# The last 64 positions of the first batch's values, loaded first as 512-byte runs on 16 partitions and summed in one block on TensorE

## Chip, cores and metric

The kernel runs on one core of one Trainium2 chip. The metric is the time of one execution on the device in microseconds (us). Nearly all executions of one kernel lie within 2 us of each other; a few are 7 to 16 us longer at a lower granted TensorE clock (0.98 or 0.99 in the mean). Those are called slow here, and only undisturbed executions are compared.

## The reference

```python
def _attn_ref(q, k, v):                    # each (8, 8, 576, 64) float32: batch, head, position, dim
    pool, scale = 8, 1.0 / np.sqrt(64)
    k_p = k.reshape(B, H, S // 8, 8, D).mean(axis=3)      # 72 pooled keys per head
    v_p = v.reshape(B, H, S // 8, 8, D).mean(axis=3)      # 72 pooled values per head
    scores = scale * np.matmul(q, k_p.transpose(0, 1, 3, 2))
    scores = scores - np.max(scores, axis=-1, keepdims=True)
    attn = np.exp(scores)
    attn = attn / (np.sum(attn, axis=-1, keepdims=True) + 1e-09)
    return np.matmul(attn, v_p)

def _moe_ref(x, w_gate, w_val, w_out):     # x (4608, 512), d_ff 1536
    return (np.maximum(x @ w_gate, 0.0) * (x @ w_val) @ w_out)

# x = the attention's output, (batch, position) as rows and (head, dim) as columns
```

The kernel casts to 16-bit floats on the way in, pools keys and values, and keeps TensorE on the feed-forward part as early and as long as it can.

## The kernel before

Two ways of pooling values are in it. For batches 2 and up, GpSimd sums eight positions with trees of adds. For the first two batches it is done on TensorE: the values lie with positions on the partitions, and a 0/1 matrix (`sel_main`, `sel_rest`) sums eight of them per output row. 576 positions are 144 runs of KG = 4 positions. 128 of these runs (512 positions) fill 128 partitions, the "main" values. The last 64 positions, the "rest", were loaded one position to a partition, on 64 partitions. In the code P = 128, SP = 72 pooled positions, HH = 4 heads (half of them), NKG = 9, and QP = 16.

```python
    def load_v_wide(b):
        tl = vin_pool.tile([P, H, POOL, D], F16, name="v_in")
        main = tl[:, :H // 2].rearrange("p h t d -> p (h t d)").rearrange(
            "p (h t d) -> p h t d", h=H, d=D)
        rest = tl[:P // 2, H // 2:].rearrange("p h t d -> p (h t) d")[:, :H]
        v_tiles[b] = (main, rest)
        nc.gpsimd.dma_start(
            out=main.rearrange("p h t d -> p h (t d)"),
            in_=v[b].rearrange("h (x t) d -> x h (t d)", t=KG)[:P])
        nc.gpsimd.dma_start(
            out=rest, in_=v[b].rearrange("h r d -> r h d")[P * KG:])
    # ... (cut)
    def warm(n):                      # dummy matmuls that keep the array busy
        ps = ps_mm.tile([P, TCH], F32, name="mm_ps", tag="mm_ps")
        for _ in range(n):
            nc.tensor.matmul(out=ps, lhsT=warm_sb[:, :P], rhs=warm_sb, start=True, stop=True)
    # ... (cut)
    def pool_v_array(b, half):
        ps = ps_mm.tile([P, HH, D], F32, name="mm_ps", tag="mm_ps")
        main, rest = v_tiles[b]
        hs = slice(half * HH, (half + 1) * HH)
        for t in range(KG):
            nc.tensor.matmul(
                out=ps[:SP], lhsT=sel_main, rhs=main[:, hs, t, :], start=(t == 0), stop=False)
        nc.tensor.matmul(
            out=ps[:SP], lhsT=sel_rest[:P // 2], rhs=rest[:, hs, :], start=False, stop=True)
        g0 = half * NG // 2
        st = stats[b % 2][:SP, g0:g0 + NG // 2, :]
        st = st.rearrange("p g (x d) -> p g x d", d=D)[:, :, 0::3, :]
        src = ps[:SP].rearrange("p (g x) d -> p g x d", x=2)
        nc.scalar.copy(st, src)       # the "cast": PSUM float32 to SBUF 16 bit
    # ... (cut) the start of the program, in this order:
        load_k_wide(0, 3)
        make_identity(nc, ident16)
        load_q(0, 0, IQ)
        load_v_wide(0)
        load_gv(0)                    # weights of the gate and value products
        load_q(0, IQ, NI - IQ)
        for i in range(1, 4):
            load_gv(i)
    # ... (cut)
        q_transposes(0, 0, nc.scalar)
        k_turn(k_ps, (3, 7, 8, 4))
        k_take(0, k_ps, False)
        k_take(0, k_ps, True)
        warm(2)
        piece_scores(0)               # exp(q k_p) of the first two pieces of 128 queries
        warm(2)
        piece_scores(1)
        warm(4)
        pool_v_array(0, 0)
        pool_v_array(0, 1)
    # ... (cut)
        values(0, 0)                  # products with the pooled values, reciprocal, multiply
        values(0, 1)
        warm(1)
        back(0, 0, nc.scalar)         # transposes into x_T, the feed-forward's input
```

Three parts further on matter for two of the experiments. GpSimd issues all loads of a batch from within its own stream of pooling adds. The third batch's q is transposed by a DMA that SP issues. VectorE forms sums of the output weights:

```python
    def q_dma(b):
        qT_tiles[b] = qT_pool.tile([P, NI, P], F16, name="qT")
        nc.sync.dma_start_transpose(
            out=qT_tiles[b], in_=q16_tiles[b].rearrange("p (i d) -> p i d", d=P))

    def prep_k(b, load_next, behind=None):
        for i in range(KJ // 2):
            run(pool_k(b, i, nc.gpsimd))              # a tree of adds
        if behind is not None:
            nc.gpsimd.tensor_copy(out=gate, in_=behind)
        if load_next:
            load_k(b + 1)
            load_q(b + 1)
            load_v(b + 1)

    def weight_sums():
        e, f = wo_sb[:, :n_hf, :HD], wo_sb[:, :n_hf, HD:]
        g, h = wo_sb[:, n_hf:, :HD], wo_sb[:, n_hf:, HD:]
        t1, t2, t3, t4 = [wo_sums[:, i] for i in range(4)]
        return [lambda o=o, x=x, y=y, i=slice(i, i + 2): nc.vector.tensor_tensor(
                    out=o[:, i], in0=x[:, i], in1=y[:, i], op=ALU.subtract)
                for o, x, y in ((t1, f, e), (t2, h, t1), (t3, h, f), (t4, g, t2))
                for i in range(0, n_hf, 2)]
```

The softmax here doesn't subtract the row's maximum and nothing guards it: scores larger than these inputs give would overflow.

## Time and profile before

| | before |
|---|---|
| time, three runs | 328.61 us median (328.54 to 330.12) |
| span in the profile | 327.4 us |
| TensorE busy | 318.7 us, 97% of the span |
| first load of q landed | 8.88 us |
| main values landed / last 64 positions landed | 12.27 / 12.75 us |
| first value product / VectorE's first reciprocal | 14.45 / 14.79 us |

The page's first part gives each engine's busy time, the chain of waits gives the work that ended last, and the timeline of one engine gives start, duration, engine, line, operation, tiles and count of each group; a bracket at a line's end is idle time just before it and what ended it. The landings come from the trace's records of the DMA engines: a load has landed when the last of its 16 engines has reported. The lines are in the prediction below. The change touches 4 to 17 us, and there TensorE sums values, ScalarE casts the sums, and VectorE takes the value products.

### The profile page before, as it was taken

The page shows a single profiled execution, that of the slowest core. Times are in us where ns is not written, and L with a number is a line of the kernel's source. Part 1 is how long each engine was busy: PE and PEld are TensorE (multiplying, and loading weights), DVE is VectorE, ACT ScalarE, POOL GpSimd, SP SyncE. Part 2 cuts the span into 40 slices and gives each one's busy share as a digit, 9 for nine tenths or more (in the row PEclk, how much of TensorE's full clock was granted, in tenths as well). Part 3 has the DMA queues.
Part 4 walks back from the last instruction along what each step waited for, and adds up shares of the span by engine and source line. Part 5 has one row for each costly group of instructions (what it writes and reads, how often), then busy time and mean ns, then how long its engine had stood idle before and what let it go on. Part 6 is the DMA issues. An engine that isn't in the chain of part 4 may idle for free.

```text
span 327.4 us, 7013 instructions
## 1 busy us (share of the span) xinstructions
PE 318.7 (97%) x2670; PEld 226.9 (69%) x2670; DVE 226.2 (69%) x482; ACT 151.2 (46%) x353; POOL 206.9 (63%) x258
## 2 busy tenths in 40 slices
PE   8899999999999999999999999999999999999995
PEld 3577885455566656665898867655667888888674
DVE  7465737677684864696387745784779989879762
ACT  1454482364466226612672257225825565565330
POOL 8556607999999942965199309999901577667300
PEclk9999999999999999999999999999999999999999
DMA  7999998996958538999794472223012130130035
GB/s 110 186 203 202 200 211 151 200 173 118 187 101 159 100 91 86 78 154 160 159 169 76 87 104 60 33 47 124 3 24 50 34 96 2 22 111 2 10 112 137
DMA packets 51010, 35.46 MB, mean 108 GB/s; under 512 B 30432, under 2 KB 45024, under 8 KB 50976
## 3 DMA queue, kind: packets, MB, share of 16 engines
q0 software_dynamic: 18304, 18.88, 36.5%
q1 hardware_dynamic: 32528, 16.00, 26.2%
q8 instruction: 21, 0.34, 0.4%
q10 hardware_dynamic: 144, 0.13, 0.1%
q14 instruction: 13, 0.11, 0.1%
HBM read 37.75 MB, written 9.44 MB: 144 GB/s over the span
## 4 chain that ended last, share of the span: by engine, by line
PE 89%; DVE 6%; DMA 2%; issue 1%; POOL 1%; ACT 0%; DVEq 0%; POOLq 0%
PE mm_ps L430 42%; PE acc_ps L523 19%; PE mm_ps L742 9%; PE at_ps L311 4%; PE mm_ps L468 3%; PE at_ps L389 3%; PE mm_ps L602 2%; DMA q<-in_q_dram 2%; PE at_ps L742 2%; DVE px L395 1%; DVE sum L514 1%; DVE h L439 1%; PE mm_ps L412 1%; PE mm_ps L366 1%; DVE px L758 1%
## 5 line engine op out<-in xcount | busy, mean ns | idle before, releaser
L439 DVE TENSOR_TENSOR h<-mm_ps,relu 128x512 f16<-128x512 f32 (+1 forms) x96 | 59.8, 624 | 69.5 <-PE mm_ps L430 59.2
L436 ACT ACTIVATE relu<-mm_ps 128x512 f16<-128x512 f32 (+1 forms) x96 | 52.2, 544 | 100.1 <-PE mm_ps L430 94.6
L430 PE MATMUL mm_ps<-x_T,wv_sb 128*128 128x512 f16 (+1 forms) x432 | 88.4, 332 | 0.4 <-DVE kpT0u L264 0.4
L430 PE MATMUL mm_ps<-x_T,wg_sb 128*128 128x512 f16 (+1 forms) x432 | 88.5, 331 | 0.0
L430 PEld LDWEIGHTS <-wv_sb 128*128 128x128 f16 x432 | 42.1, 98 | 31.2 <-DVE kpT0u L264 0.8
L430 PEld LDWEIGHTS <-wg_sb 128*128 128x128 f16 x432 | 38.9, 97 | 19.7 <-issue 0.3
L325 ACT ACTIVATE expT<-at_ps 72x288 f16<-72x288 f32 (+2 forms) x128 | 38.8, 374 | 14.3 <-PE at_ps L311 14.2
L523 PEld LDWEIGHTS <-sum 128*128 128x128 f16 x336 | 32.0, 98 | 6.3 <-DVE sum L514 0.9
L395 DVE TENSOR_TENSOR px<-at_ps,prd 128x256 f16<-128x256 f32 (+1 forms) x80 | 33.8, 423 | 2.7
L181 POOL TENSOR_TENSOR tree_b<-tree_a 72x256 f32<-72x256 f32 (+1 forms) x42 | 33.5, 797 | 3.3
L764 POOL TENSOR_TENSOR h<-px 128x256 f16<-128x256 f16 x36 | 25.4, 718 | 13.8 <-ACT px L761 12.8
L175 POOL TENSOR_TENSOR tree_a<-k_in 96x512 f32<-96x512 f16 x18 | 21.5, 1196 | 15.2 <-DMA k_in<-in_k_dram 15.2
L523 PE MATMUL acc_ps<-wo_sums,sum 128*128 128x256 f16 x252 | 30.9, 272 | 0.0
L175 POOL TENSOR_TENSOR tree_a<-v_in 72x512 f32<-72x512 f16 x24 | 28.7, 1197 | 0.1
L523 PEld LDWEIGHTS <-h 128*128 128x128 f16 x252 | 23.7, 98 | 2.9
L763 POOL TENSOR_SCALAR px<-px 128x256 f16<-128x256 f16 x12 | 13.0, 1080 | 18.1 <-PE mm_ps L742 15.3
L844 POOL COPY gate<-h 128x1 f16<-128x1 f16 x4 | 1.5, 380 | 33.9 <-DVE h L439 33.9
L523 PE MATMUL acc_ps<-wo_sb,h 128*128 128x256 f16 x168 | 20.6, 272 | 0.0
L514 DVE TENSOR_TENSOR sum<-h 128x768 f16<-128x768 f16 x28 | 19.0, 679 | 0.0
L531 DVE TENSOR_TENSOR rows<-acc_ps,mid 128x512 f32<-128x512 f32 x21 | 14.4, 686 | 4.7 <-PE acc_ps L523 4.6
L389 PEld LDWEIGHTS <-expT 72*128 72x128 f16 (+1 forms) x280 | 12.9, 100 | 5.9 <-DVE prd L394 0.8
L394 DVE RECIPROCAL prd<-at_ps 128x4 f32<-128x4 f32 (+1 forms) x80 | 13.7, 171 | 3.7 <-PE at_ps L389 3.6
(144 smaller groups left out, 527.9 us busy)
## 6 DMA issues: line engine op xcount, KB each, us to landing
out_dram<-rows SPq DMA_DIRECT2D x24, 256.0 KB
k_in<-in_k_dram POOLq DMA_DIRECT2D x7, 576.0 KB, 7.0
q<-in_q_dram POOLq DMA_DIRECT2D x7, 576.0 KB, 10.0
v_in<-in_v_dram POOLq DMA_DIRECT2D x6, 576.0 KB, 12.7
wg_sb<-in_moe_w_gate_dram POOLq DMA_DIRECT2D x6, 256.0 KB, 11.0
wv_sb<-in_moe_w_val_dram POOLq DMA_DIRECT2D x6, 256.0 KB, 10.8
wo_sb<-in_moe_w_out_dram POOLq DMA_DIRECT2D x3, 512.0 KB, 10.7
v_in<-in_v_dram POOLq DMA_DIRECT2D x2, 512.0 KB, 11.9
```

Of the source, the lines that this page charges most:

```text
L175: eng.tensor_tensor(out=cell["a"][:n], in0=src[:, :, :4 * D], in1=src[:, :, 4 * D:], op=ALU.add)
L181: eng.tensor_tensor(out=cell["c"][:n], in0=a[:n, :, :2 * D], in1=a[:n, :, 2 * D:], op=ALU.add)
L325: nc.scalar.activation(out=out_ap, in_=in_ap, func=AF.Exp, scale=EXP_SCALE)
L389: nc.tensor.matmul(out=ps[:n, c0:c0 + D + 1], lhsT=weights(b, h, t), rhs=stats[b % 2][:SP, g, s0:s0 + D + 1], start=True, stop=True,)
L395: nc.vector.tensor_tensor(out=x[:n, half * NG // 2:(half + 1) * NG // 2, :, :], in0=pv.rearrange("p g (x c) -> p g x c", x=2)[:, :, :, :D] ...
L430: nc.tensor.matmul(out=t[:, lo:hi], lhsT=w[:, ci, fsl], rhs=x_T[:, ci, x0:x0 + hi - lo], start=(ci == 0), stop=(ci == n_co - 1),)
L436: nc.scalar.activation(out=relu[:, :n], in_=ps[0][:, :n], func=AF.Relu)
L439: nc.vector.tensor_tensor(out=h_tiles[c][:, fo, t0:t0 + n], in0=ps[1][:, :n], in1=relu[:, :n], op=ALU.mult)
L514: nc.vector.tensor_tensor(out=S[k][:, i], in0=x[:, i], in1=y[:, i], op=op)
L523: nc.tensor.matmul(out=ps[:, tb, :], lhsT=lhs[:, i, tb * P:(tb + 1) * P], rhs=rhs[:, i, :], start=(first and tb == 0 and i == 0), stop=(tb ...
L742: nc.tensor.matmul(out=ps[key][:, m], lhsT=w_of(m)[:, i], rhs=xs[:, i], start=(first and m == 0 and i == 0), stop=(m == 1 and i == N_CO - ...
L764: nc.gpsimd.tensor_tensor(out=hc[:, fo_out, cols], in0=gv[:, 0], in1=gv[:, 1], op=ALU.mult)
```

## The change

The intent: rest and main values should come in the order in which the array can use them. The rest goes ahead, as runs of four positions (512 bytes) on 16 partitions, and is summed for both halves in one block behind the scores; two of the four dummy matmuls go, since there is now real work; then follow the main values.

```diff
--- before.py
+++ after.py
@@ -86,6 +86,7 @@
 
     sel_main = const_pool.tile([P, SP], F16, name="sel_main")
     sel_rest = const_pool.tile([P, SP], F16, name="sel_rest")
+    sel_runs = const_pool.tile([P, SP], F16, name="sel_runs")
     kg = const_pool.tile([P, QT * 2 // POOL, 2 * D], F16, name="kg")
     warm_sb = const_pool.tile([P, TCH], F16, name="warm_sb")
 
@@ -151,13 +152,18 @@
         tl = vin_pool.tile([P, H, POOL, D], F16, name="v_in")
         main = tl[:, :H // 2].rearrange("p h t d -> p (h t d)").rearrange(
             "p (h t d) -> p h t d", h=H, d=D)
-        rest = tl[:P // 2, H // 2:].rearrange("p h t d -> p (h t) d")[:, :H]
+        runs = v[b].rearrange("h (x t) d -> x h (t d)", t=KG)
+        if b:
+            rest = tl[:P // 2, H // 2:].rearrange("p h t d -> p (h t) d")[:, :H]
+        else:
+            rest = tl[:QP, H // 2:].rearrange("p h t d -> p (h t d)").rearrange(
+                "p (h t d) -> p h t d", h=H, d=D)
+            nc.gpsimd.dma_start(out=rest.rearrange("p h t d -> p h (t d)"), in_=runs[P:])
         v_tiles[b] = (main, rest)
-        nc.gpsimd.dma_start(
-            out=main.rearrange("p h t d -> p h (t d)"),
-            in_=v[b].rearrange("h (x t) d -> x h (t d)", t=KG)[:P])
-        nc.gpsimd.dma_start(
-            out=rest, in_=v[b].rearrange("h r d -> r h d")[P * KG:])
+        nc.gpsimd.dma_start(out=main.rearrange("p h t d -> p h (t d)"), in_=runs[:P])
+        if b:
+            nc.gpsimd.dma_start(
+                out=rest, in_=v[b].rearrange("h r d -> r h d")[P * KG:])
 
     def load_q(b, i0=0, n=NI):
         if b not in q16_tiles:
@@ -333,16 +339,30 @@
         c0 = NF * P if t == n_pc - 1 else (HS + RI * QP if j else 0) + n_blk * P
         return exp_tiles[b, h][:SP, c0:c0 + n]
 
-    def pool_v_array(b, half):
+    def pool_v_rest(half):
 
         ps = ps_mm.tile([P, HH, D], F32, name="mm_ps", tag="mm_ps")
+        rest = v_tiles[0][1][:, half * HH:(half + 1) * HH]
+        for t in range(KG):
+            nc.tensor.matmul(
+                out=ps[:SP], lhsT=sel_runs[:QP], rhs=rest[:, :, t, :], start=(t == 0),
+                stop=False)
+        return ps
+
+    def pool_v_array(b, half, ps=None):
+
+        first = ps is None
+        if first:
+            ps = ps_mm.tile([P, HH, D], F32, name="mm_ps", tag="mm_ps")
         main, rest = v_tiles[b]
         hs = slice(half * HH, (half + 1) * HH)
         for t in range(KG):
             nc.tensor.matmul(
-                out=ps[:SP], lhsT=sel_main, rhs=main[:, hs, t, :], start=(t == 0), stop=False)
-        nc.tensor.matmul(
-            out=ps[:SP], lhsT=sel_rest[:P // 2], rhs=rest[:, hs, :], start=False, stop=True)
+                out=ps[:SP], lhsT=sel_main, rhs=main[:, hs, t, :], start=(first and t == 0),
+                stop=(not first and t == KG - 1))
+        if first:
+            nc.tensor.matmul(
+                out=ps[:SP], lhsT=sel_rest[:P // 2], rhs=rest[:, hs, :], start=False, stop=True)
         g0 = half * NG // 2
         st = stats[b % 2][:SP, g0:g0 + NG // 2, :]
         st = st.rearrange("p g (x d) -> p g x d", d=D)[:, :, 0::3, :]
@@ -893,6 +913,7 @@
             nc.vector.memset(st[:SP, :, D:3 * D], ONE)
         nc.vector.memset(sel_main, 0.0)
         nc.vector.memset(sel_rest, 0.0)
+        nc.vector.memset(sel_runs, 0.0)
         load_k_wide(0, 3)
         make_identity(nc, ident16)
         load_q(0, 0, IQ)
@@ -910,6 +931,7 @@
         for sel, at, m, i, src in (
                 (sel_main, slice(0, P), slice(0, 7), slice(0, NKG), ident16[:, :126]),
                 (sel_main, slice(0, P), slice(7, 8), slice(0, 1), ident16[:, 126:]),
+                (sel_runs, slice(0, QP), slice(7, 8), slice(1, NKG), ident16[:QP, :QP]),
                 (sel_rest, slice(0, 64), slice(7, 8), slice(1, NKG), ident16[:64, :64])):
             out_ap = sel.rearrange("p (i m) -> p m i", i=NKG)[at, m, i]
             nc.vector.tensor_reduce(
@@ -931,9 +953,10 @@
         piece_scores(0)
         warm(2)
         piece_scores(1)
-        warm(4)
-        pool_v_array(0, 0)
-        pool_v_array(0, 1)
+        v_ps = [pool_v_rest(half) for half in range(2)]
+        warm(2)
+        pool_v_array(0, 0, v_ps[0])
+        pool_v_array(0, 1, v_ps[1])
 
         half = TCH // 2
         a = [lambda fo=fo: gate_val(0, fo, 0, half) for fo in range(n_fo)]
```

The second batch keeps the old form: there `ps` is None.

## The prediction

> **What bounds the kernel now.** I read the page's busy shares first, then the chain of work that ended last, then the waits by engine, then the timeline of the only stretch that the change touches (about 4 to 17 us), engine by engine. The page says which engine sets the time:
>
> ```profile
> PE 318.7 (97%) x2670; PEld 226.9 (69%) x2670; DVE 226.2 (69%) x482; ACT 151.2 (46%) x353; POOL 206.9 (63%) x258
> ...
> PE 89%; DVE 6%; DMA 2%; issue 1%; POOL 1%; ACT 0%; DVEq 0%; POOLq 0%
> ```
>
> TensorE is busy for 97% of the span and holds 89% of the chain; only 2% of the chain is DMA, and the chain in order of time puts all of it into one piece at the start, the first load of q (3.62 us, for 5.26 us). The pooled values of the first batch come soon after. The chain around them:
>
> ```profile
> 12.21 0.86 PE mm_ps L245 x4
> 13.07 0.44 PE mm_ps L342 x4
> 13.51 0.23 PE mm_ps L344
> 13.73 0.56 PE mm_ps L342 x4
> 14.29 0.23 PE mm_ps L344
> 14.52 0.24 PE at_ps L389 x4
> ...
> 14.79 0.19 DVE prd L394
> ```
>
> L245 are dummy matmuls (`warm`) that keep the array busy while data is on its way. L342 sums the 512 main positions of the values, L344 the last 64, L389 are the first value products, and from 14.79 VectorE's four reciprocal-and-multiply pairs run back to back until 17.08. Nothing in this chain is a DMA: the values are there when TensorE wants them. TensorE's own timeline says the same:
>
> ```profile
> 12.04 1.03 PE L245 MATMUL mm_ps<-warm_sb 128*128 128x512 f16 x4
> 12.91 0.60 PE L342 MATMUL mm_ps<-v_in,sel_main 128*72 128x256 f16 x4
> 13.44 0.30 PE L344 MATMUL mm_ps<-v_in,sel_rest 64*72 64x256 f16 x1
> 13.66 0.63 PE L342 MATMUL mm_ps<-v_in,sel_main 128*72 128x256 f16 x4
> 14.22 0.30 PE L344 MATMUL mm_ps<-v_in,sel_rest 64*72 64x256 f16 x1
> 14.45 0.30 PE L389 MATMUL at_ps<-stat,pexp 72*128 72x65 f16 x4
> ```
>
> No row here carries an idle time that a load ended. In the trace's records of landings, the last of 16 engines reported the main values at 12.27 us (their first weight load, the next in its stride, started at 12.69) and the last 64 positions at 12.75 (first used at 13.44). So both loads have slack, 0.4 and 0.7 us. ScalarE and GpSimd in the same stretch:
>
> ```profile
> 13.77 0.37 ACT L350 CAST stat<-mm_ps 72x256 f16<-72x256 f32 x1 [0.59 <-PE mm_ps L344]
> 14.55 0.37 ACT L350 CAST stat<-mm_ps 72x256 f16<-72x256 f32 x1 [0.42 <-PE mm_ps L344]
> ```
> ```profile
> 12.55 0.74 POOL L825 DMA_DIRECT2D wv_sb<-in_moe_w_val_dram  x1 [2.51 <-DMA v_in<-in_v_dram]
> ```
>
> The two casts move the sums of half 0 and half 1 (four heads each) to SBUF; the value products need them. GpSimd's 2.51 us of waiting is for a lane of the DMA semaphores and is off the chain.
>
> [...] each L344, with 64 rows instead of 128, costs more than its slot (worked out below). [...] 106 ns for the 64-row load of 72 columns, 109 to 113 for the 128-row ones. So 16 rows are not cheaper than 64. [...] from 10.5 to 12.4 us, where the 512 packets of 128 B run among 512 B ones, the queue moved 184 GB/s, from 8.5 to 10.5 us, with 512 B alone, 166. [...]
>
> **The change part by part.**
>
> *Loads.* The 64 positions become 128 runs of 512 B (before: 512 of 128 B), queued ahead of the main values. The bytes are the same 64 KB, which at 184 GB/s are 0.36 us. The queue is a line: q lands at 8.88, so the 64 positions should land by about 9.3 (before 12.75), and the main values at 12.27 + 0.36 = 12.6.
>
> *VectorE.* One memset and one small reduction more. The reductions start 0.06 us apart and end at 4.56; the next instruction waits for k until 4.83. Some 0.1 us more fits in that gap: 0.
>
> *GpSimd.* Its semaphore lanes follow the order of issue, so the weight load that was held until 12.55 now waits for the small load, and goes at about 10.05. The queue moves 166 to 200 GB/s all the time anyway, so an earlier place at its end brings no earlier landing: 0.
>
> *TensorE, removed and added.* Spacing from the timeline: four warm matmuls in 1.03 us at 379 ns each start (1.03 - 0.379)/3 = 0.217 us apart; four L342 in 0.60 at 273 ns start 0.109 apart. From the first warm matmul (12.04) to the first value product (14.45) are 2.41 us: 4 x 0.217 + 8 x 0.109 + 2 x 0.109 = 1.96, so the two visits to the 64-row shape cost the remaining 0.45, or 0.22 each. After: 2 warm (0.43), 8 main (0.87), 8 of the 16-row kind (two half tiles x four positions, 0.87 if they stream like the others) and one visit to another shape, since all eight stand together (0.22): 2.40. TensorE would be ready for the value products at 14.44. The sum is a tie: eight matmuls come for two, and two warm ones and one switch go.
>
> *The wait that comes with it.* Before, L344 and the second half stood between the end of half 0 (13.44 + 0.30 = 13.74) and the value products (14.45), 0.71 us in which the cast of half 0 (to 14.14) was hidden. After, half 0 ends with its fourth main matmul, and only the four of half 1 follow. It starts at 14.44 - 5 x 0.109 = 13.90 and ends at 14.17; cast from 14.21 (0.04 later, as before) to 14.58; the product follows 0.05 later (as the second cast's, 14.92 to 14.97): 14.63. That is 0.18 us later than 14.45. The cast of half 1 ends at about 15.05, its products at 15.3, ahead of VectorE's second pair at about 15.5, so it adds nothing. VectorE's pairs, the transposes and everything behind them move by the 0.18. Sum: +0.2 us on 328.61, 328.8.
>
> **The rivals.**
>
> *A wait on the last 64 positions goes away.* That seems to be the intent. It needs executions in which they land after 13.3; this profile has them 0.6 us ahead. GpSimd's wait speaks for late values, but at 12.3. If true of the timed runs, some tenths: 328.3.
>
> *The 16-row matmuls do not stream.* If each showed its weight load, as the lone L344 does (297 ns), eight would cost 8 x (0.297 - 0.109) = 1.5 us more: 330.3. Against it: four transposes with 64 rows follow each other 0.03 us apart at 51.3 us, after one switch.
>
> *The main values come too late.* They stand behind the small load. [...] Their first matmul is now at about 13.56, because the small sums and two warm ones are ahead of it. [...] It would take over 1.3 us of delay to matter.
>
> *The cast is hidden after all*, if the switch back costs more before the main sums and everything ends later anyway, or less: between -0.1 and +0.2.
>
> **Range and chances.** The stretch that changes lasts 2.41 us; 2% of the time are 6.6 us, so even its removal is within 2%. Losses over 2% would need a load several us late[...]. The three runs before differ by 1.6 us (328.54 to 330.12), though two by 0.07. I take 328.8, with 328.0 to 329.6 for the rivals of a few tenths and the scatter; faster 0.01, within 2% 0.98, slower 0.01.
>
> **What would show it.** In the profile after: the small sums in one block of eight about 0.109 apart behind a gap of some 0.1 us, starting near 12.1; main sums from about 13.55 with no load named ahead of them; an idle time of TensorE before the first value product ended by the first cast; VectorE's first reciprocal near 14.97 instead of 14.79. A first reciprocal before 14.7, spacing near 0.3 in the small sums, or an idle time ended by the load of the values would prove a step wrong. A time outside 328.0 to 329.6 would mean a cost outside this stretch that I haven't seen.

Cut from it, where marked, are rules that no trace of this case shows, and in the third rival an estimate that rested on one (main values at 12.9 us, a slack of 0.7). None of them is a term of the sum, which stands as it was made: 0 for the loads, VectorE and GpSimd, a tie on TensorE (2.40 for 2.41 us) and +0.18 for the exposed cast, so +0.2 us on 328.61, 328.8. Without the cut estimate, the main values of 12.6, wanted at 13.56, have a slack of about 1.0 us. Three things that it says in passing are in the two traces. The queue as a line: the first eight loads landed in the order of their issue (before at 4.81, 5.72, 7.63, 8.88, 12.27, 12.75, 13.98 and 15.32 us). The semaphores: GpSimd's loads signal eight of them in turn, 99 to 106, so that the 13th load and the fifth share 103; before, the 13th was issued at 12.55 behind the fifth, the main values, landed at 12.27. The weight load of 16 rows: 104 to 108 ns in the profile after, for 106 with 64 rows.

## The result

| | before | after |
|---|---|---|
| time, fast runs | 328.88 us median of 4 (328.54 to 330.12) | 329.66 us median of 4 (329.10 to 330.07) |
| ratio after / before | | 1.0018, 95% interval 0.9995 to 1.0040: the same |
| two later comparisons of the same kernel | | 1.0010 (0.9986 to 1.0034); 0.9998 (0.9984 to 1.0012) |
| span in the profile | 327.4 us | 327.5 us |

A ratio is the mean time of one kernel's fast runs over the mean of the other's in the same rounds, so it is not quite the ratio of the medians. The times say "within 2%" and nothing finer: the three intervals all hold the predicted 1.0005, and 1.0000 too. The rest has to be read in the trace.

The page after: the busy times are those of before to 0.3 us, and TensorE has four matmuls more (two dummies and two 64-row ones gone, eight 16-row ones come).

```profile
PE 318.4 (97%) x2674; PEld 227.1 (69%) x2674; DVE 226.0 (69%) x484; ACT 151.4 (46%) x353; POOL 206.6 (63%) x258
...
PE 88%; DVE 6%; DMA 2%; issue 1%; ACT 1%; POOL 1%; DVEq 0%; ACTq 0%; POOLq 0%
```

TensorE's timeline after, the answer to the one in the prediction:

```profile
11.86 1.06 PE L347 MATMUL mm_ps<-v_in,sel_runs 16*72 16x256 f16 x8
12.86 0.60 PE L251 MATMUL mm_ps<-warm_sb 128*128 128x512 f16 x2
13.30 1.04 PE L360 MATMUL mm_ps<-v_in,sel_main 128*72 128x256 f16 x8
14.35 0.28 PE L409 MATMUL at_ps<-stat,pexp 72*128 72x65 f16 x4
```

The eight small sums stand in one block, 0.109 us apart like the main ones. Everything starts about 0.27 us earlier than in the profile before only because q landed at 8.61 instead of 8.88 us in this execution. So the two traces have to be laid on each other at a common event before the change. I take the last score matmul of the second piece, which starts at 11.99 before and at 11.71 after. From it:

| from the start of the last score matmul to | before | after | difference |
|---|---|---|---|
| end of TensorE's work for the sums (next matmul could start) | 14.45 - 11.99 = 2.46 | 13.30 + 8 x 0.109 - 11.71 = 2.46 | 0.00 |
| first value product | 2.46 | 14.35 - 11.71 = 2.64 | +0.18 |
| first reciprocal (called D from here on) | 2.80 | 2.96 | +0.16 |

What the product waits for is in ScalarE's timeline after:

```profile
13.94 0.80 ACT L370 CAST stat<-mm_ps 72x256 f16<-72x256 f32 x2 [1.02 <-PE mm_ps L360]
```

The two casts run back to back from 13.94. The first ends 0.37 us after its start, at about 14.31, and the product follows at 14.35, while TensorE was ready at 14.17. Before, the first cast began at 13.77 and was over long before the product at 14.45. By the records of landings, the rest lands at 9.09 us instead of 12.75, the main values at 12.35 instead of 12.27. GpSimd's timeline after shows that its wait moved one load on, from the weights at 12.55 to the next (on semaphore 103 is now the rest, on 104 the main values):

```profile
9.86 0.81 POOL L845 DMA_DIRECT2D wv_sb<-in_moe_w_val_dram  x1
12.63 0.75 POOL L845 DMA_DIRECT2D wg_sb<-in_moe_w_gate_dram  x1 [1.97 <-DMA v_in<-in_v_dram]
```

### The profile page after: what moved, and what is told of

It reads as the page before. It is cut to its first block, busy times and chain, and to the rows that moved or that the text cites. A ratio compares the mean times of both kernels' runs of the same rounds, so it can differ in the third digit from the quotient of the medians.

```text
span 327.5 us, 7023 instructions
## 1 busy us (share of the span) xinstructions
PE 318.4 (97%) x2674; PEld 227.1 (69%) x2674; DVE 226.0 (69%) x484; ACT 151.4 (46%) x353; POOL 206.6 (63%) x258
## 4 chain that ended last, share of the span: by engine, by line
PE 88%; DVE 6%; DMA 2%; issue 1%; ACT 1%; POOL 1%; DVEq 0%; ACTq 0%; POOLq 0%
PE mm_ps L450 42%; PE acc_ps L543 19%; PE mm_ps L762 9%; PE at_ps L317 4%; PE mm_ps L488 3%; PE at_ps L409 3%; PE mm_ps L622 2%; PE at_ps L762 2%; DMA q<-in_q_dram 2%; DVE px L415 1%; DVE sum L534 1%; DVE h L459 1%; PE mm_ps L432 1%; DVE px L778 1%; PE mm_ps L288 1%
## 5 line engine op out<-in xcount | busy, mean ns | idle before, releaser
L187 POOL TENSOR_TENSOR tree_b<-tree_a 72x256 f32<-72x256 f32 (+1 forms) x42 | 32.6, 776 | 3.3
L181 POOL TENSOR_TENSOR tree_a<-k_in 96x512 f32<-96x512 f16 x18 | 20.7, 1150 | 13.1 <-DMA k_in<-in_k_dram 13.1
L534 DVE TENSOR_TENSOR sum<-h 128x768 f16<-128x768 f16 x28 | 18.9, 676 | 0.0
L409 PEld LDWEIGHTS <-expT 72*128 72x128 f16 (+1 forms) x280 | 12.9, 100 | 5.9 <-DVE prd L414 0.8
```

Of the source, the lines that this page charges most:

```text
L181: eng.tensor_tensor(out=cell["a"][:n], in0=src[:, :, :4 * D], in1=src[:, :, 4 * D:], op=ALU.add)
L187: eng.tensor_tensor(out=cell["c"][:n], in0=a[:n, :, :2 * D], in1=a[:n, :, 2 * D:], op=ALU.add)
L409: nc.tensor.matmul(out=ps[:n, c0:c0 + D + 1], lhsT=weights(b, h, t), rhs=stats[b % 2][:SP, g, s0:s0 + D + 1], start=True, stop=True,)
L534: nc.vector.tensor_tensor(out=S[k][:, i], in0=x[:, i], in1=y[:, i], op=op)
```

## The experiments

**Theory:** the exchange on TensorE is a tie, the loads are off the path, and the only new cost is that the first cast is no longer hidden: +0.16 to +0.18 us up to the first reciprocal. **Rivals:** small changes of this stretch reach the end in another size than 1:1 (something later swallows or enlarges them), or the loads' order did gain something that something else took back.

D is the measure below, since it does not depend on when q landed; "later" is the time from the first reciprocal to TensorE's last matmul. Before: D 2.80, later 308.33. After: 2.96 and 308.66.

### The same kernel again (e1, e9), and the kernel before again (e8)

No edit.

> The changed kernel again, unaltered. D is the time from the start of the last score matmul of the second piece to VectorE's first reciprocal; it was 2.80 us in the kernel before and 2.96 in the changed one. Theory (the exposed cast of half 0 costs 0.16 us and nothing else of the change counts): D 2.96 again, ratio to before 1.0005, so about 0.2 us, with scatter of some tenths from elsewhere. Rival (something outside the stretch costs more, as the first timing's 1.0018 suggests): D 2.96 and a ratio of 1.0015 to 1.002 again.

Five of the six runs were fast (328.37 to 329.70), ratio 1.0010 (0.9986 to 1.0034), but the one with the profile was slow: 343.77 us, granted clock 0.98. Its D of 3.41 cannot be compared.

> The kernel before, unaltered, for a second trace of it. Theory: D 2.80 within 0.02, while the landing of q and the time from the first reciprocal to the last matmul (308.33 us in the first trace) move by some tenths from execution to execution; so the 0.33 us by which the changed kernel's trace was longer in that part is scatter. Rival: 308.33 again, and the changed kernel costs 0.3 us in a later place.

The execution that was looked at took 337.55 us, again a slow one, so what I expected of an undisturbed one was not tested here. It does show what this slow execution consists of. q landed at 9.69 us; TensorE's timeline has the wait for it, and the table of windows (length, then busy time and count of PE, PEld, DVE, ACT, POOL, then clock, DMA share and GB/s) the clock afterwards:

```profile
9.74 0.62 PE L282 MATMUL mm_ps<-ident,q 128*128 128x128 f16 x8 [1.83 <-DMA q<-in_q_dram]
```
```profile
11.00:15.00 4.00, 3.53 (x22) 2.41 (x22) 1.29 (x4) 2.56 (x5) 2.06 (x3) 0.57 1.51 197
...
73.00:77.00 4.00, 3.99 (x17) 2.05 (x17) 0.48 (x1) 1.32 (x5) 3.54 (x5) 0.57 0.94 184
```

In the trace's clock records the clock is halved from 11.57 to 14.98, 3.41 us, and again from 73.0 to 76.4. Ahead of the first stretch TensorE had been idle for 1.83 us in one piece and some 0.5 us besides. In the undisturbed trace of the kernel before, the wait for q was 0.92 us, and the granted clock stayed at 1.00.

The second stretch follows a wait of 4.3 us for the third batch's transposed q (in the waits by engine), to which I come back with e7. So the record holds one undisturbed trace of the kernel before; its D is checked again with e7, e11 and e12, which differ from it in this stretch by dummies alone.

> The changed kernel a third time, for a second undisturbed trace and five more rounds. Theory: D 2.96 within 0.02; the time from the first reciprocal to the last matmul somewhere between 308.0 and 308.7, the spread of the traces so far; ratio to before 1.0005, with the interval holding 1. Rival (a systematic cost later on): 308.66 again and a ratio near 1.0015.

Five fast runs, 329.05 us median, ratio 0.9998 (0.9984 to 1.0012), and a profile of a fast one. D is 2.957 us, against 2.959 in the first: the +0.16 repeats to 0.002 us (so it does in e6 and e10 below, which sum in the same order: 2.959 in both). "Later" is 307.78, 0.88 us less than in the other trace of the very same kernel. So the time behind the changed stretch scatters by several times the effect. All 14 fast runs of the changed kernel together have a mean of 329.24 us, the 24 of the kernel before 328.95: +0.29, with a standard error of about 0.18 by the scatter of single runs (0.5 us in each). That fits +0.2 and does not prove it.

### The dummy matmuls moved between the halves (e2)

```diff
-        warm(2)
         pool_v_array(0, 0, v_ps[0])
+        warm(2)
         pool_v_array(0, 1, v_ps[1])
```

> The changed kernel with its two warm matmuls moved between the main sums of half 0 and half 1. Same instructions on every engine. Theory (the cast of half 0 is exposed because only four matmuls stand behind half 0): the cast is hidden, the idle time ended by the first cast is gone, D 2.78 (0.18 less), as in the kernel before. Rival (the 0.16 us come from the number or shape of the matmuls): D stays 2.96.

TensorE's timeline of e2:

```profile
12.95 0.60 PE L360 MATMUL mm_ps<-v_in,sel_main 128*72 128x256 f16 x4 [0.17 <-DMA v_in<-in_v_dram]
13.38 0.59 PE L251 MATMUL mm_ps<-warm_sb 128*128 128x512 f16 x2
13.82 0.60 PE L360 MATMUL mm_ps<-v_in,sel_main 128*72 128x256 f16 x4
14.25 0.29 PE L409 MATMUL at_ps<-stat,pexp 72*128 72x65 f16 x4
```

The cast of half 0 now runs from 13.58 to 13.95, under the two dummies and half 1, and the product follows half 1 with no wait: the theory's new wait is gone, with the same instructions. But D is 3.00, not smaller. The bracket in the first line says why: in this execution the main values landed at 12.91, and without the dummies ahead of them they were wanted at about 12.71, so some 0.24 us were lost there; 3.00 - 0.24 = 2.76, and the kernel before has 2.80. The time (329.45, one of the six runs slow; ratio of the fast ones 1.0017, 0.9994 to 1.0039) tells nothing. What follows: the cast is what the product waited for. Hiding it works only where the main values come early enough, so the two dummies in the changed kernel stand in a place that covers the load.

### All dummies of this stretch away (e3, e4)

e3 takes `warm(2)` out of the changed kernel, e4 `warm(4)` out of the kernel before.

```diff
         v_ps = [pool_v_rest(half) for half in range(2)]
-        warm(2)
         pool_v_array(0, 0, v_ps[0])
```
```diff
         piece_scores(1)
-        warm(4)
         pool_v_array(0, 0)
```

> The changed kernel without the two warm matmuls. Theory (no load is waited for): main sums start 0.43 us earlier, D 2.53, no idle time ended by a load. Rival (the warm matmuls cover a wait for the main values): idle time of TensorE before the first main sum, D 2.7 to 2.96.

> The kernel before without its four warm matmuls. Theory: the loads are nearly there; the main values land about 0.25 us after TensorE is free for them, so of the 0.87 us taken away some 0.6 are won: D about 2.2, less than any form with the small sums first (2.53 without warm matmuls). Rival (the intent of the change: the last 64 positions come too late in this order): a wait of TensorE at the sum of the last 64 positions, D 2.6 or more.

TensorE's timeline of e4:

```profile
12.50 0.63 PE L342 MATMUL mm_ps<-v_in,sel_main 128*72 128x256 f16 x4
13.06 0.30 PE L344 MATMUL mm_ps<-v_in,sel_rest 64*72 64x256 f16 x1
13.29 0.63 PE L342 MATMUL mm_ps<-v_in,sel_main 128*72 128x256 f16 x4
13.84 0.30 PE L344 MATMUL mm_ps<-v_in,sel_rest 64*72 64x256 f16 x1
14.07 0.30 PE L389 MATMUL at_ps<-stat,pexp 72*128 72x65 f16 x4
```

In e3 the main sums follow the small ones directly (13.04 behind 12.05), the first value product starts at 14.12, and D is 2.54, 0.42 less than after, the two dummies' 2 x 0.217 = 0.43. In e4 it is 2.25, 0.54 less than before, though four dummies would be 0.87: here the main values, landed at 12.46, became what TensorE waited for (first sum at 12.50). In each the first value product leaves earlier, and in each the time does not follow: 328.81 us, ratio 1.0000 (0.9979 to 1.0021), and 328.74 us, 1.0004 (0.9976 to 1.0031). The intervals are wide enough to hold 0.4 us, so I also compared the traces matmul by matmul, as a difference of starts against the kernel before. Behind the changed stretch e3 was 0.35 us ahead, e4 0.24. From 65 us on they were 0.17 and 0.15 ahead. At 65 us TensorE waits for a copy by VectorE that stands behind two adds of the output weights' sums. The second add took 1.22 us in e3 and 1.13 in e4, against 1.03 before, so what was given back there fits the length of an add and is no fixed share of a gain.

By the same comparison the changed kernel's +0.16 (0.27 us ahead at q, 0.11 ahead from 15.5 us on) stays the same up to 65 us: until there the stretch's cost passes on 1:1. All the traces say so: from the first reciprocal to the first of those adds, near 61 us, there are 45.98 to 46.00 us in 11 of the 14, with D anywhere from 2.54 to 6.25, and at most 46.12 in the others. At 65 us the changed kernel waited 0.18 us where the kernel before had waited 0.35, and gained 0.17: its second add took 0.86 us and not 1.03. At 117 us it lost 0.48 (from 0.28 ahead to 0.20 behind), with a wait for VectorE's rows, ahead of which one add had taken 1.36 us and not 0.81. VectorE's timeline before, and after:

```profile
114.78 0.81 DVE L514 TENSOR_TENSOR sum<-h,sum 128x768 f16<-128x768 f16 x1
```
```profile
114.50 1.36 DVE L534 TENSOR_TENSOR sum<-h,sum 128x768 f16<-128x768 f16 x1
```

The other trace of the changed kernel (e9) lost nothing there. So this is no step of the change, but scatter of executions. Where it comes from is asked with e10.

### Two visits to the 16-row shape instead of one (e5)

```diff
-        v_ps = [pool_v_rest(half) for half in range(2)]
-        warm(2)
+        v_ps = [pool_v_rest(0)]
+        warm(1)
+        v_ps.append(pool_v_rest(1))
+        warm(1)
```

> The changed kernel with the small sums parted: half 0, one warm matmul, half 1, one warm matmul. The same instructions, but two visits to the 16-row shape instead of one. Theory (a visit costs about 0.22 us, as the remainder in the prediction says): D 2.96 + 0.22 = 3.18. Rival (the change of shape costs nothing, the remainder has another cause): D 2.96.

TensorE's timeline of e5:

```profile
11.93 0.62 PE L347 MATMUL mm_ps<-v_in,sel_runs 16*72 16x256 f16 x4
12.48 0.39 PE L251 MATMUL mm_ps<-warm_sb 128*128 128x512 f16 x1
12.80 0.62 PE L347 MATMUL mm_ps<-v_in,sel_runs 16*72 16x256 f16 x4
13.36 0.39 PE L251 MATMUL mm_ps<-warm_sb 128*128 128x512 f16 x1
13.58 1.04 PE L360 MATMUL mm_ps<-v_in,sel_main 128*72 128x256 f16 x8
```

D is 3.183 us, against 2.959 after: +0.224 for one more visit, as expected. The price of a change of the tile's shape, which the prediction had taken as a remainder of the old timeline (0.22), is now measured by itself. The main values landed late in this execution (13.33) and were still not waited for, since their first sum stood at 13.58. One look, 329.51 us.

### The main values loaded ahead of the rest (e6)

```diff
-            nc.gpsimd.dma_start(out=rest..., in_=runs[P:])
+            nc.gpsimd.dma_start(out=main..., in_=runs[:P])
+            nc.gpsimd.dma_start(out=rest..., in_=runs[P:])
```

(shortened; the later `dma_start` of main is then skipped for the first batch)

> The changed kernel with the main values loaded ahead of the last 64 positions again; the sums stay as changed, small ones first. Theory: the last 64 positions then land about 3.7 us after q, 0.6 us after the last score matmul, so TensorE waits some 0.4 to 0.5 us at the first small sum and D is 3.3 to 3.5: the order of loading is needed by the order of summing, and by nothing else. Rival (the order of loading makes no difference): D 2.96.

A miss: D is 2.959, exactly that of the changed kernel, and no sum waits for a load (the small sums start at 12.59, the main ones at 14.02). The rest landed at 12.34, but in this execution q had landed late, at 9.33, so that the last score matmul started only at 12.44. In the other undisturbed traces with the small sums these began between 11.7 and 12.2; with a rest that lands at 12.34 they would have waited, but no run shows it. So the run does not show what the order of the loads is worth when q is on time; that stays open. It does show that the old order would have been harmless in this execution.

### How much a delay of this stretch costs at the end (e7, e11, e12)

The dummies of the kernel before were raised from 4 to 20 (e7) and to 10 (e11), a delay that is known: 16 x 0.217 = 3.47 us and 6 x 0.217 = 1.30 us.

```diff
         piece_scores(1)
-        warm(4)
+        warm(20)          # e11: warm(10)
         pool_v_array(0, 0)
```

> The kernel before with 20 warm matmuls instead of 4 ahead of the sums: 16 x 0.217 = 3.47 us more on the chain at this place. Theory A (a delay here goes through to the end): D 6.27 and 3.4 us more, ratio 1.0105. Theory B (part of it is given back where TensorE waits for VectorE later, near 65 us): D 6.27, ratio between 1.005 and 1.009.

D grew by 3.46 us to 6.25, as it should. But the time was 340.15 us (four runs from 340.02 to 340.41), ratio 1.0346 (1.0317 to 1.0374), 11 us more, three times the delay. Both theories missed. The waits by engine of e7 and SP's own queue have the rest:

```profile
PE at_ps L311 <- DMA qT<-q: 6.1, 1, 6.1
```
```profile
57.88 11.98 SPq L292 DMA_TRANSPOSE qT<-q  x1
```

In the kernel before, the same line of SP reads

```profile
54.69 4.42 SPq L292 DMA_TRANSPOSE qT<-q  x1
```

SP was with the transposing load of the third batch's q for 11.98 us instead of 4.42, and by the records of landings it was complete 17.2 us after its issue instead of 9.2. TensorE waited 6.1 us for it, and 2.56 us into that idle time the clock was halved, from 71.5 to 78.3 us. What lies beside it differs: GpSimd issues the fourth batch's loads behind its own adds, whose place in time the dummies don't move. In e7 that is at 56.95, ahead of SP's 57.88; in the kernel before at 57.80, when the transposing load had been under way for 3.1 us. My new theory: the other loads, issued first or close behind, are what makes it slow. e12 tests it. It keeps the 20 dummies, but gives GpSimd a reason to wait: a tiny copy that reads the transposed q, ahead of those loads. (`prep_k` has an argument for it.)

```diff
-        prep_k(2, True)
+        prep_k(2, True, qT_tiles[2][:, 0, :1])
```

First for e11, then for e12:

> The kernel before with 10 warm matmuls instead of 4: 6 x 0.217 = 1.30 us more. Theory (the 11 us that 20 warm matmuls cost are 3.3 us of delay and a step of 6 us or more where the transposing load of the third batch's queries comes to run beside GpSimd's loads of the fourth batch): 1.3 us do not reach the step, no idle time of TensorE near 66 us, D 4.10, ratio 1.003 to 1.004. Rival (every delay at the start is multiplied by about three): 4 us, ratio 1.012.

> The kernel with 20 warm matmuls, and GpSimd's loads of the fourth batch held back until the transposing load of the third batch's queries has landed (a copy of one column that waits for it). Theory of the step: the transposing load runs alone, TensorE's wait of 6.1 us for it near 68 us falls below 1 us, and the ratio is about 1.010 to 1.014 instead of 1.035. Rival (the transposing load is late in itself, not slowed by the loads beside it): the wait stays at 6 us and the ratio at 1.035 or more.

e11: D 4.09 (+1.30), 330.57 us, ratio 1.0048 (1.0033 to 1.0064), or +1.6 us for 1.30: no wait of TensorE between 55 and 100 us, and no multiplication. It is a step and not a slope. e12: D 6.25 again, and 333.03 us, ratio 1.0122 (1.0108 to 1.0135), +4.0 us for 3.45. The GpSimd and SP timelines of e12:

```profile
63.89 0.19 POOL L844 COPY gate<-qT 128x1 f16<-128x1 f16 x1 [6.95 <-DMA qT<-q]
64.13 0.58 POOL L127 DMA_DIRECT2D k_in<-in_k_dram  x1
```
```profile
57.95 4.35 SPq L292 DMA_TRANSPOSE qT<-q  x1
```

With the same 20 dummies and the fourth batch's loads held until 64.13, the transposing load is back at 4.35 us, the 6.1 us wait of TensorE is gone, and so are 7 of the 11 us. Less their dummies, D is 2.79 in e11 and 2.78 in e7 and e12, the 2.80 of the kernel before within 0.02. That settles e7. All the traces fit it, when the lead of the transposing load (GpSimd's first load of the fourth batch, less SP's issue) is set beside its time from issue to landing:

| trace | lead, us | issue to landing, us | TensorE's wait for it, us |
|---|---|---|---|
| e12, loads held | 6.2 | 5.9 | none |
| before, after, e2, e3, e4, e5, e9 | 2.0 to 3.6 | 8.3 to 10.1 | none |
| e6, e11 | 1.4, 1.5 | 10.6, 10.8 | none |
| e8, e1 (slow executions) | 0.6, 0.5 | 15.8, 20.0 | 4.3, 8.5 |
| e7 | -0.9 | 17.2 | 6.1 |
| e10 (below) | -5.0 | 29.9 | 18.9 |

The time is not in step with the lead at the short end (20.0 at 0.5, 17.2 at -0.9), but between leads of 1.4 and 0.6 us it jumps by 5 us. Only e7 against e12 moves the loads at will, and there GpSimd's adds behind the loads are held back with them; but in e10 (below) those adds are gone and the transposing load is slowest of all, so it is the loads. The other rows agree with it. "Later" is 308.81 here and 308.14 in e11, against 308.33 before and 316.20 in e7: a delay in this stretch is passed to the end 1:1, give or take the scatter of some 0.5 us, unless it takes the lead from SP's transposing load. It also gives the second half of a slow execution like e8's: a late q, a halved clock, a start late by some 2.5 us, and so a lead of 0.6 us.

### No summing trees on GpSimd (e10, a wrong result)

```diff
-            run(pool_k(b, i, nc.gpsimd))
+            pass
...
-            run(pool_v(b, g, nc.gpsimd))
+            pass
```

(and one memset of the untouched tile, so that nothing uninitialised is read; relative error 1.23, as intended)

> Wrong results on purpose: the changed kernel without GpSimd's summing trees for keys and values from the third batch on (the loads stay). Theory (VectorE's 16-bit adds are stretched when GpSimd computes at the same time, and that is what scatters the later part): the adds of the output weights' sums, 0.43 to 1.03 us each in the traces so far, all take about 0.43, and the longest sum of two hidden tiles between 85 and 165 us falls from over 1.3 us to about 0.8. Rival (the stretching has another cause, as the data or the DMA): they keep their spread.

The whole time is of no use, 349.35 us: without its adds GpSimd issues the fourth batch's loads early (the first at 49.95 us, for 57.80 before), and TensorE waits 18.9 us for the transposing load of q. That is e7's step once more, and further along. But VectorE's adds answer the question. The groups by tile, with minimum, median and maximum in ns ahead of the stretch in which they lie, before and in e10:

```profile
L494 DVE TENSOR_TENSOR wo_sums<-wo_sb x6: 416/499/1106, 60.8 to 77.0; 128x512 f16<-128x512 f16 x6
L494 DVE TENSOR_TENSOR wo_sums<-wo_sb,wo_sums x6: 416/674/894, 67.0 to 82.9; 128x512 f16<-128x512 f16 x6
```
```profile
L514 DVE TENSOR_TENSOR wo_sums<-wo_sb x6: 415/415/416, 61.0 to 98.0; 128x512 f16<-128x512 f16 x6
L514 DVE TENSOR_TENSOR wo_sums<-wo_sb,wo_sums x6: 415/415/419, 66.7 to 103.5; 128x512 f16<-128x512 f16 x6
```

The same twelve instructions take 415 to 419 ns when GpSimd adds nothing, and 416 to 1106 beside its trees. The longest sum of two hidden tiles between 85 and 165 us falls from 1.93 us in the changed kernel to 0.55, further than the 0.8 that I expected: the 0.81 shown above was itself a stretched one. From 218 us on GpSimd adds in e10 too (other work than the trees), and there such sums again take up to 1.50 us. So all of the scatter of those twelve is gone with the trees; whether GpSimd's adds are stretched in turn was not examined. The kept traces show it add by add as well. In before, after and e9 together, the 80 of VectorE's 240 adds of these two kinds that no arithmetic instruction of GpSimd overlaps take at most 0.55 us, and all 98 that take over 0.6 us overlap one. The add of 1.36 us at 114.50 is among them; GpSimd's add of 1.15 us began at 114.29. Which of VectorE's adds is hit differs between executions of one kernel. That this makes up the whole scatter of 307.8 to 308.7 in "later" is likely, but not shown.

## Why the prediction was right, point by point

- *"Nothing in this chain is a DMA"; both loads have slack.* Right. After, no sum waits for a value. The predicted landings, by about 9.3 and 12.6 us, were 9.09 and 12.35, and 9.31 and 12.65 in e9. The slack of the main values is smaller than I said in unlucky executions: 13.33 in e5, against 13.3 to 13.6 when they are wanted.
- *VectorE and GpSimd cost nothing.* Right. The added memset and reduction take 0.09 and 0.20 us and VectorE still waits 0.28 us for k behind them (0.27 before). The weight load was issued at 9.86, for 10.05 predicted, and the wait moved to the load behind it.
- *TensorE is a tie, 2.41 against 2.40.* Right to 0.01: 2.46 us on either side from the last score matmul. Its pieces hold as well: 0.109 spacing in the small sums, and 0.224 us for a visit to another shape, in e5 by itself.
- *The cast of half 0 is no longer hidden, +0.18.* Right: +0.18 at the first value product and +0.16 at the first reciprocal, in two traces; e2 with the same instructions in another order has no such wait.
- *"VectorE's first reciprocal near 14.97", "starting near 12.1".* The figures on the clock of the trace were 14.67 and 11.86, and by the test I had set, a reciprocal before 14.7 would have proved a step wrong. It doesn't: q landed 0.27 us earlier in this execution. Measured from the last score, the figure is 14.79 + 0.16 = 14.95. The mistake was to give an absolute time for a stretch that follows a load which lands anywhere from 8.47 to 9.33 us in the undisturbed traces.
- *"Everything behind them move by the 0.18."* Right up to 61 us, by the comparison matmul by matmul and the constant 46.0 us from the first reciprocal to the first add. Behind that, VectorE's stretched adds move the end by up to 0.9 us between executions, and the timing can't resolve the rest. e11 and e12 show that larger delays are passed on.
- *328.8 us, from 328.0 to 329.6.* The first median, 329.66, is 0.06 above; the later ones, 329.05 and 329.4 with a slow run (329.17 without it), are inside. The kernel before rose by 0.27 with a fourth run as well; 328.61 x 1.0018 would be 329.2. I had said that a time outside would mean a cost outside this stretch. By the traces, what was outside is the scatter just named and not a cost of the change: e9's trace has less of it than the kernel before. The times alone (+0.29, standard error 0.18) don't settle it. Part of it is the base that I started from: 328.61, the median of three runs, lies 0.34 below the mean of all 24 fast runs of that kernel.

Of the rivals, the wait for the rest that goes away was not there in the one undisturbed trace of before, nor in e4, where no dummies stand ahead of the sums; the 16-row sums do stream (0.109 us apart); the main values were not too late. What nobody gains by is the early landing of the rest, by 3.66 us: it was not waited for. No version here beats both kernels. e4 has the smallest D, 0.54 us less than before, and its time is not measurably different.

## What to carry to other kernels

A load that comes earlier is worth its wait and no more (here the last 64 positions came 3.66 us earlier and nothing was gained): look for an idle time which that load ended, and if there is none, count what the new order does to the engines, above all which casts and copies lost the work that hid them. Between two traces of different executions, measure from a common event just ahead of the change, or the landing of the first load (0.27 us apart here) passes for an effect. And a delay at the start can cost more than itself: here 1.30 us cost 1.6, and 3.47 us cost 11, since that one brought two engines' loads together that had been apart; ask what is issued next to what, later on.

## What was measured of the hardware here

- A visit of one to eight matmuls to a 64- or 16-row shape and back cost 0.22 us: 0.45 us for the two visits in the timeline of before, and +0.224 us of D for one more (e5).
- Among 512-byte packets, 512 packets of 128 B cost nothing visible: before, the queue moved 184 GB/s with them (10.5 to 12.4 us) and 166 without (8.5 to 10.5 us). And turning them into 512-byte runs on 16 partitions gained nothing that was waited for.
- The clock was halved in e8 for 3.41 us after TensorE had been idle for 1.83 us in one piece and some 0.5 us besides, and for 3.41 us again at the end of a wait of 4.3 us; in e7 for 6.8 us, from 2.56 us into a wait of 6.1 us. With waits of 0.92 us (before) and 0.95 us (e12) the granted clock was 1.000. What decides it was not shown.
- A transposing load issued by SP, with plain loads that GpSimd issued ahead of it or up to 0.6 us behind it, took 15.8 to 29.9 us to its landing (e1, e7, e8, e10); with a lead of 1.4 to 3.6 us it took 8.3 to 10.8, and with those loads held 5.9 (e12).
- Whether the 16 partitions slow a load is not decided here. The 64 KB landed 0.48 us after q in the profile after, and from 0.31 to 0.66 in the six other traces that load them first; my estimate at the rate of before was 0.36.
